# Turning q and k of two first blocks on quarters of the array, with their loads and two M1 chunks moved

## The chip, the cores and the metric

The kernel runs on one core of one Trainium2 chip. Its time is the device time of an execution in microseconds (us). Of the kernel before, three runs are shown; the median is 339.99 us. The engines are PE (TensorE, the 128x128 matmul array, with its weight loads shown as PEld), DVE (VectorE), ACT (ScalarE), POOL (GpSimd) and SP (SyncE, which here only issues DMAs). The pages' "L583" is line 583 of the kernel before.

## What is computed

For 8 batches, 8 heads, 576 positions and 64 values a head, a causal attention with forgetting, and then a two-layer SiLU network on the 4608 rows of 512 values:

```python
scores = scale * np.matmul(q, k.transpose(0, 1, 3, 2))
cum = np.cumsum(np.log(np.clip(f, 0.0001, 1.0)), axis=-1)
decay = cum[:, :, :, None] - cum[:, :, None, :]
scores = np.where(causal, -1000000000.0, scores + decay)
attn = softmax(scores)
x = (attn @ v), heads side by side          # 4608 x 512
h = x @ w_in                                # 512 x 2048
out = (h / (1 + exp(-h))) @ w_out           # 2048 x 512
```

The forgetting factor of the key is folded into v (and into a column of ones beside it, which gives the denominators); that of the query cancels in the division.

## The kernel before

**Two kinds of attention work.** The first 128 positions of each batch are its *first block*. They are worked on ahead of everything else, a whole batch of 8 heads at once: `load_qk0` (two POOL-queue DMAs per batch, one for q and one for k, each 128 rows of 512 values, cast to bf16 on the way, row = 16 position groups x 8 heads), `turn0` (turns them so that the head's 64 values lie on the partitions), `scores0`, `mask0`, `out0`, `back0`. Positions 128 to 575 are worked on in the main loop in 32 *pairs* of heads: `load_qk`, `cast_qk` (POOL), a DMA transpose on SP's queue (`transposes`, L443), `scores` (L475), `mask`, `attend` (L522, L531), `back`.

**`turn0`** takes q or k of one batch. For each of 8 positions c in a group and each j of two head halves it does one matmul (L293): the 128 rows x 64 values as weights, a 128x64 selection matrix `sel[:, j, :]` as the moving operand, the result on partitions 64j to 64j+63 of a tile `tp` in the PSUM pool `pbig` (4 buffers of one bank, shared with the tiles of M1, M2 and others). ACT copies q's tile out to `qT0`, DVE copies k's to `kT0`. A batch has 32 of these matmuls. The score tiles are in another PSUM pool, `psc` (2 buffers of two banks).

**M1 and M2** are the two layers of the network. The rows are cut into 10 groups; group 0 is the first blocks of batches 0 to 3 (512 rows), groups 1 and 2 those of batches 4, 5 and 6, 7 (256 rows each). An M1 chunk (`m1_chunk`, L583) is 4 matmuls, tanh on ACT (L591) and one DVE operation (L592); a group has 16. An M2 part (`m2_part`, L628) is 4 matmuls of 512 columns on a quarter of w_out; four parts make 128 rows of output, which ACT scales (L638) and SP stores (L607). In the main loop some M2 work has another form (`m2_rows`, L654).

**What sets the order.** All engines run in the order in which the program is written. Between the pieces of attention, `fill(us)` asks a planner (`wanted`, `plan`) for M1 chunks and M2 parts worth so many microseconds by the planner's own costs, and `step(kind)` asks for one. Before the main loop the order is: turns of batches 0 to 3 and their attention; M1 chunks of group 0; `two_more(4)` (turns, scores, output of batches 4 and 5, with fills between); a list of kinds written out by hand (1 is an M1 chunk, 2 an M2 part); `fill(2.2)`; `two_more(6)`; stores and loads; `fill(4.2)`; the main loop. `two_more(6)` begins with four `turn0`, then two steps of fill, then `scores0` of both batches.

**The loads.** Two queues matter. POOL's, in this order: q and k of the first blocks, v of them, w_in in quarters, w_out in quarters (`load_w_out(0)` to `(3)`), with POOL's own conversions of v (`convert_v0`) between them; the last ones before the main loop are `load_qk0(6)`, `load_qk0(7)`, `load_v0(6)`, `load_v0(7)`. And SP's: everything for the main loop. SP's queue begins with `after(...)` (L211), a tiny DMA that waits for the second quarter of w_out; then q, k, tails, transposes, v and stores in the program's order.

Of the kernel before, what the change touches and what calls it, by code (L numbers as in the profile page):

```python
# [10 lines left out]
FP32 = mybir.dt.float32  # L11
BF16 = mybir.dt.bfloat16
P = 128
# [5 lines left out]
def kernel(  # L19
# [10 lines left out]
    nc = tc.nc  # L30

    B, H, S, D = q.shape
# [4 lines left out]
    NP = H // 2  # L37
# [10 lines left out]
    RUN = 8  # L48
    NRUN = P // RUN
    assert D == 64 and S == 576 and DM == H * D and NP == NCC and B == 8  # L50
    assert NRUN * H == P
    scale = 1.0 / float(D) ** 0.5

    ctx.enter_context(tc.manual_schedule(engines=set(ORDERED)))
# [1 line left out]
    const = ctx.enter_context(tc.tile_pool(name="const", bufs=1))  # L56
    stage = ctx.enter_context(tc.tile_pool(name="stage", bufs=1))
    conv = ctx.enter_context(tc.tile_pool(name="conv", bufs=6))
    qktp = ctx.enter_context(tc.tile_pool(name="qktp", bufs=4))
# [8 lines left out]
    psc = ctx.enter_context(tc.tile_pool(name="psc", bufs=2, space=bass.MemoryType.PSUM))  # L68
# [4 lines left out]
    w_bf = const.tile([P, NM + 1, BH], BF16, name="w_bf")  # L73
    ident_bf = const.tile([P, P], BF16, name="ident_bf")
    sel = const.tile([P, 2, D], BF16, name="sel")
    ident_f = const.tile([BH, BH], FP32, name="ident_f")
    tri = const.tile([P, P], BF16, name="tri")
    trit = const.tile([P, 2, ST], BF16, name="trit")
# [4 lines left out]
    kT0 = [const.tile([P, NP, P], BF16, name=f"kT0_{b}") for b in range(B)]  # L83
# [46 lines left out]

    def load_qk0(b):
        t = conv.tile([P, 2, RUN * D], BF16, name="qkb", tag="qkb")
        for i, src in enumerate((q, k)):
            nc.gpsimd.dma_start(
                out=t[:, i, :],
                in_=src[b, :, 0:P, :].rearrange("h (r c) d -> r h (c d)", c=RUN),
            )
        qk0[b] = t

    def load_v0(b):  # L140
# [62 lines left out]
    def load_w_out(i):  # L203
        c0, c1 = i * NFC // WQ, (i + 1) * NFC // WQ
        nc.gpsimd.dma_start(
            out=w_out_bf[:, c0:c1, :],
            in_=moe_w_out[c0 * P : c1 * P, :].rearrange("(fc p) m -> p fc m", p=P),
        )
# [22 lines left out]
    for i in range(2):  # L231
        nc.vector.tensor_copy(
            out=sel[:, i, :].rearrange("p (a r) -> p a r", a=NP),
            in_=ident_bf[:, :].rearrange("p (r i a) -> p i a r", i=2, a=NP)[:, i, :, :],
        )

    def keep_warm(n):
# [7 lines left out]
        out=f_sb[:, :], in0=f_sb[:, :], scalar1=1e-4, scalar2=1.0, op0=ALU.max, op1=ALU.min  # L245
# [39 lines left out]
    def turn0(b, i):  # L285
        src = qk0[b]
        if i == 0:
            qT0[b] = qktp.tile([P, NP, P], BF16, name="qT0", tag="qT0", bufs=2)
        dst, evac = ((qT0[b], nc.scalar.copy), (kT0[b], nc.vector.tensor_copy))[i]
        tp = pbig.tile([P, NP, NRUN, RUN], FP32, name="tp", tag="big")  # L290
        for c in range(RUN):
            for j in range(2):
                nc.tensor.matmul(  # L293
                    tp[j * D : (j + 1) * D, :, :, c].rearrange("p a r -> p (a r)"),
                    lhsT=src[:, i, c * D : (c + 1) * D],
                    rhs=sel[:, j, :],
                    start=True,
                    stop=True,
                )
        evac(  # L300
            out=dst[:, :, :].rearrange("p a t -> p (a t)"),
            in_=tp[:, :, :, :].rearrange("p a r c -> p (a r c)"),
        )
# [43 lines left out]
    def convert_v0(b):  # L347
        nc.gpsimd.tensor_tensor(
            out=v0[b][:, :, :],
            in0=vf0.pop(b)[:, :, :],  # L350
            in1=w_bf[:, 0, b * H : (b + 1) * H, None].to_broadcast([P, H, D + 1]),
            op=ALU.mult,
        )
# [85 lines left out]
    def transposes(n):  # L439
        src = qbf.pop(n)  # L440
        t = qktp.tile([P, NX, P], BF16, name="qkT", tag="qkT")
        qkT[n] = t[:, :, :].rearrange("p x c -> p (x c)")
        nc.sync.dma_start_transpose(  # L443
            out=t[:, :, :], in_=src[:, :, :].rearrange("p x c -> p (x c)")
        )
# [130 lines left out]
    def m1_chunk(g, fc):  # L576
        w = GW[g]
        if fc == 0:
            gts[g] = gpools[g % 3].tile([P, NFC, w], BF16, name="gt", tag=f"gt{g % 3}")
        gt = gts[g]  # L580
        hp = pbig.tile([P, w], FP32, name="hp", tag="big")
        for cc in range(NCC):
            nc.tensor.matmul(  # L583
                hp[:, :],
                lhsT=w_in_bf[:, cc, fc * P : (fc + 1) * P],
                rhs=xcols(g, cc),
                start=(cc == 0),
                stop=(cc == NCC - 1),
            )
        th = tpool.tile([P, w], BF16, name="th", tag="th")  # L590
        nc.scalar.activation(out=th[:, :], in_=hp[:, :], func=ACT.Tanh, scale=0.5)  # L591
        nc.vector.scalar_tensor_tensor(  # L592
            out=gt[:, fc, :],
            in0=th[:, :],
            scalar=1.0,
            in1=hp[:, :],
            op0=ALU.add,
            op1=ALU.mult,
        )
# [95 lines left out]
    def wanted(a, c):  # L695


        g1 = M1[a][0] if a < len(M1) else NG
        g2 = M2[c][0] if c < len(M2) else NG
        can1 = g1 in ready and not (M1[a][1] == 0 and g1 > g2 + lag["g"])  # L700
        can2 = open2["w"] and c < len(M2) and g2 < g1
        if can1 and can2 and lag["parts"]:
            return 2 if sum(M2_OF[:g1]) - c > lag["parts"] else 1
        if not can1 or not can2:
            return 1 if can1 else 2 if can2 else 0
        a0, c0 = begin.get(g1, (M1[a][1], c)) if M1[a][1] else (0, c)
        c1 = sum(M2_OF[:g1])
        f1 = (M1[a][1] - a0 + 0.5) / (NFC - a0)
        f2 = (c - c0 + 0.5) / max(1, c1 - c0)
        return 1 if f1 <= f2 else 2  # L710

    def step(force=0):

        a, c = at["m1"], at["m2"]
        want = wanted(a, c)
        if not want:
            return None
        g1 = M1[a][0] if a < len(M1) else NG
        g2 = M2[c][0] if c < len(M2) else NG
        can1 = g1 in ready and not (M1[a][1] == 0 and g1 > g2 + lag["g"])  # L720
        can2 = open2["w"] and c < len(M2) and g2 < g1
        kind = force if (force == 1 and can1) or (force == 2 and can2) else want
        if kind == 1:
            if M1[a][1] == 0:
                begin[g1] = (0, c)
            m1_chunk(g1, M1[a][1])
            at["m1"] += 1
            t = 4 * (GW[g1] / 2.4 + 2.5)
        else:
            m2_part(*M2[c])  # L730
            at["m2"] += 1
            t = 4 * (DM / 2.4 + 2.5)
        return t
# [20 lines left out]
    def fill(us_, least=0, ends=(0, 0)):  # L754

        left = us_ + at["left"]
        kinds = plan(left)
        kinds += [0] * (least - len(kinds))
        if any(ends) and kinds:
            if 2 not in kinds:  # L760
                kinds[0] = 2
            n1, n2 = len(kinds) - kinds.count(2), kinds.count(2)
            e0 = 1 if ends[0] else 0
            e1 = 1 if ends[1] and n2 > e0 else 0
            inner = n2 - e0 - e1
            n = n1 + inner
            mid = [2 if (x + 1) * inner // n > x * inner // n else 1 for x in range(n)]
            if inner and mid[-1] == 2 and e1 and not e0:
                mid = mid[::-1]
            kinds = [2] * e0 + mid + [2] * e1  # L770
        for k in kinds:
            t = step(k)
            if t is None:
                at["left"] = 0.0
                return
            left -= t / 1000
        at["left"] = left
# [48 lines left out]
    for i in range(2):  # L826
        r = slice((1 - i) * ST, (2 - i) * ST)
# [2 lines left out]
        nc.gpsimd.memset(t[:, 0:NM, 1, :], 0.0)  # L830
    load_w_out(0)
    load_w_out(1)
    convert_v0(4)
    convert_v0(5)
    load_w_out(2)
    load_w_out(3)
    load_qk0(6)
    load_qk0(7)
    load_v0(6)
    load_v0(7)  # L840
# [11 lines left out]
    cast_qk(1)  # L852
    transposes(1)

    def two_more(b):
        for x in range(2):
            turn0(b + x, 0)
            turn0(b + x, 1)
        fill(1.2, 2)
        for x in range(2):  # L860
            scores0(b + x)
            mask0(b + x)
        fill(2.6 if b == 4 else 3.4, 3)
        out0(b)
        fill(0.6, 1)
        out0(b + 1)
        fill(0.8, 2)
        back0(b, on_act)
        fill(0.6, 1)
        back0(b + 1, on_act)  # L870
        if b == 4:
            open2["w"] = True
            step(2)
        else:
            fill(0.6, 1)
# [1 line left out]
    fill(5.9)  # L877
    two_more(4)
    ready.add(1)
    for kind in (1, 1, 2, 1, 1, 2, 1, 1, 1, 1, 2):  # L880
        assert step(kind) is not None
    at["left"] = 0.0
    begin[M1[at["m1"]][0]] = (M1[at["m1"]][1], at["m2"])
    fill(2.2)
    two_more(6)
    ready.add(2)
    store(len(stores))
# [6 lines left out]
    for c in range(NM):  # L894
        convert_v(0, c)
    fill(4.2)

# [80 lines left out]
    for m in range(NQ):  # L980
# [19 lines left out]
        if m > 0:  # L1000
            if m % 2 == 0:
                b = m // 2 - 1
# [90 lines left out]
```

## Time and profile before

| | us |
|---|---|
| three runs | 340.03, 339.99, 338.6 (median 339.99) |
| the profiled execution | 341.14 |
| its span, first to last instruction | 339.4 |
| PE busy | 326.7 |
| ACT, DVE, POOL busy | 217.2, 200.5, 139.5 |
| granted PE clock | 0.999 |

A timeline row gives the start in us, the time covered, the engine, the line, the operation with its operands (out<-in), and how many instructions were merged; in square brackets, the engine's idle time before it and what ended it. "SPq" is SP's queue issuing a DMA. Rows of the chain of waits give start, duration, and what the end of the program hung on at that time. In the page's second part each digit stands for a fortieth of the span, 8.5 us, and gives the busy share in tenths. The trace also has each DMA's landing, from the semaphore that it raises; where a text gives a landing, it is that record.

The stretches that matter here, in us from the span's start: first blocks of batches 0 to 3 until 18.6; M1 of group 0 and batches 4 and 5 until 37.5; M1 of group 1 with M2 of group 0 and, from 47.4, batches 6 and 7, until 62.4; then the main loop.

### The profile page before, as it was taken

How to read it: one execution, taken by the hardware profiler on the slowest of the kernel's cores; microseconds unless marked ns; L12 is line 12 of the kernel's file. 1: busy time of each engine (PE TensorE's matmuls, PEld its weight loads, DVE VectorE, ACT ScalarE, POOL GpSimd, SP SyncE). 2: the span in 40 equal slices, each digit the busy share in tenths (PEclk: the TensorE clock that was granted, in tenths of full speed). 3: DMA queues.
4: the chain of work that ended last, by engine and by line, in shares of the span. 5: the costliest groups of instructions: out<-in, count | busy, mean ns of one | idle time of the engine just before them, and what ended most of it. 6: DMA issues, size and time to landing. Idle time of an engine off the chain costs nothing.

```text
span 339.4 us, 10334 instructions
## 1 busy us (share of the span) xinstructions
PE 326.7 (96%) x4268; PEld 229.2 (68%) x4292; DVE 200.5 (59%) x435; ACT 217.2 (64%) x385; POOL 139.5 (41%) x223
## 2 busy tenths in 40 slices
PE   7999999999999999999999997999999999999995
PEld 3745566798786767758857894867676676555654
DVE  4668745369568467565656965886673557344330
ACT  5767546687777577758748792866776486344431
POOL 8894426574764664464474352628060000000000
PEclk9999999999999999999999999999999999999999
DMA  8999999999999998997999789959973110001012
GB/s 155 187 189 220 180 215 164 241 171 172 182 188 170 168 186 158 194 190 150 181 179 165 147 148 147 156 115 188 151 108 87 53 38 33 34 33 59 34 62 63
DMA packets 144703, 48.01 MB, mean 141 GB/s; under 512 B 133328, under 2 KB 139728, under 8 KB 144656
## 3 DMA queue, kind: packets, MB, share of 16 engines
q1 hardware_dynamic: 115088, 36.60, 56.9%
q0 software_dynamic: 29408, 10.62, 27.0%
q8 instruction: 33, 0.54, 0.7%
q10 hardware_dynamic: 160, 0.13, 0.2%
q14 instruction: 14, 0.11, 0.1%
HBM read 36.85 MB, written 9.44 MB: 136 GB/s over the span
## 4 chain that ended last, share of the span: by engine, by line
PE 85%; DMA 6%; DVE 4%; POOL 2%; issue 1%; ACT 1%; SPq 1%; POOLq 0%
PE hp L583 33%; PE po L628 20%; PE pr L654 15%; PE sc L475 6%; PE dn L522 5%; DMA vf<-in_v_dram 3%; PE dn L531 2%; DMA qkb<-in_k_dram 1%; PE tp L293 1%; DVE gt L592 1%; DMA qf<-in_q_dram 1%; DVE ut L498 1%; DVE u L343 1%; SPq L443 1%; POOL vp L429 1%
## 5 line engine op out<-in xcount | busy, mean ns | idle before, releaser
L591 ACT ACTIVATE th<-hp 128x384 bf16<-128x384 f32 (+2 forms) x208 | 96.5, 468 | 75.0 <-PE hp L583 68.8
L592 DVE SCALAR_TENSOR_TENSOR gt<-th,hp 128x384 bf16<-128x384 bf16 (+2 forms) x208 | 107.5, 523 | 54.3 <-ACT th L591 44.3
L583 PE MATMUL hp<-x,w_in_bf 128*128 128x384 bf16 (+2 forms) x701 | 120.6, 321 | 0.7 <-DVE gt L592 0.4
L583 PEld LDWEIGHTS <-w_in_bf 128*128 128x128 bf16 x832 | 79.0, 98 | 50.2 <-issue 3.7
L486 ACT ACTIVATE u<-sc 128x1024 bf16<-128x1024 f32 (+1 forms) x96 | 74.3, 811 | 6.9 <-PE sc L475 6.9
L628 PE MATMUL po<-w_out_bf,gt 128*128 128x512 bf16 (+1 forms) x316 | 74.1, 368 | 1.4 <-DVE gt L592 0.2
L654 PE MATMUL pr<-w_out_bf,gt 64*128 64x256 bf16 x1024 | 61.4, 269 | 0.0
L409 POOL CAST qkb<-qf 128x384 bf16<-128x384 f32 x32 | 17.3, 542 | 88.9 <-DMA qf<-in_q_dram 88.3
L654 PEld LDWEIGHTS <-gt 64*128 64x128 bf16 x1024 | 51.2, 94 | 3.9
L628 PEld LDWEIGHTS <-gt 128*128 128x128 bf16 x336 | 32.2, 98 | 27.4 <-issue 0.3
L160 POOL DMA_DIRECT2D qkb<-in_k_dram x56 | 43.9, 786 | 0.8 <-issue 0.7
L429 POOL TENSOR_TENSOR vp<-vf,w_bf 128x520 bf16<-128x520 f32 (+1 forms) x40 | 36.5, 915 | 14.0 <-DMA vf<-in_v_dram 11.9
L638 ACT ACTIVATE osb<-po 128x512 f32<-128x512 f32 (+1 forms) x21 | 12.1, 577 | 26.5 <-PE po L628 26.5
L475 PE MATMUL sc<-qkT 64*128 64x128 bf16 (+1 forms) x640 | 28.2, 206 | 0.4 <-DMA qkT<-qkb 0.3
L492 DVE TENSOR_TENSOR u<-u,tri 128x768 bf16<-128x768 bf16 x32 | 20.2, 631 | 13.5 <-ACT u L486 13.5
L475 PEld LDWEIGHTS <-qkT 64*128 64x128 bf16 x640 | 20.3, 94 | 7.6 <-issue 4.7
L480 ACT ACTIVATE ut<-sc 128x640 bf16<-128x640 f32 x32 | 22.4, 701 | 3.0 <-PE sc L475 2.5
L522 PEld LDWEIGHTS <-u 128*128 128x128 bf16 x576 | 20.6, 97 | 3.1
L522 PE MATMUL dn<-vp,u 128*128 128x65 bf16 x384 | 21.8, 193 | 0.0
L540 DVE TENSOR_TENSOR xr<-dn,rec 128x448 bf16<-128x448 f32 x32 | 20.0, 625 | 1.1
L522 PE MATMUL dn<-v,u 128*128 128x65 bf16 x192 | 20.0, 194 | 0.0
L665 DVE COPY fence<-pr 128x1 f32<-128x1 f32 x16 | 2.5, 158 | 28.0 <-PE pr L654 28.0
(70 smaller groups left out, 243.4 us busy)
## 6 DMA issues: line engine op xcount, KB each, us to landing
out_dram<-osb SPq DMA_DIRECT2D x32, 256.0 KB, 2.9
vf<-in_v_dram SPq DMA_DIRECT2D x26, 256.0 KB, 5.1
qf<-in_q_dram SPq DMA_DIRECT2D x64, 96.0 KB, 3.3
qkb<-in_k_dram POOLq DMA_DIRECT2D x56, 48.0 KB, 4.0
w_in_bf<-in_moe_w_in_dram POOLq DMA_DIRECT2D x4, 512.0 KB, 6.8
w_out_bf<-in_moe_w_out_dram POOLq DMA_DIRECT2D x4, 512.0 KB, 9.1
vf<-in_v_dram POOLq DMA_DIRECT2D x6, 256.0 KB, 9.6
qkb<-in_q_dram POOLq DMA_DIRECT2D x8, 128.0 KB, 4.9
```

Source lines behind the costliest of these rows:

```text
L160: nc.gpsimd.dma_start(out=t2[:, NR + 1 : NX, j * D : (j + 1) * D], in_=k[b, head(p, j), P:SM, :].rearrange("(c p) d -> p c d", p=P),)
L429: nc.gpsimd.tensor_tensor(out=vbf[b][ro, c, ho, :], in0=vst[b][c][r, h, :], in1=w.to_broadcast([r.stop - r.start, h.stop - h.start, D + 1] ...
L475: nc.tensor.matmul(sc[:, i, o : o + q1 - q0], lhsT=kt, rhs=t[r, q0:q1], start=True, stop=True)
L480: nc.scalar.activation(out=ut[:, :, 0:3:2, :].rearrange("p k i t -> p i k t"), in_=sc[:, :, T0 : T0 + (NM + 1) * ST].rearrange("p i (k t) ...
L486: nc.scalar.activation(out=u[:, :, c * SM : c * SM + w], in_=sc[:, :, 0:w], func=ACT.Exp, scale=scale)
L492: nc.vector.tensor_tensor(out=x, in0=x, in1=tri[:, None, None, :].to_broadcast([P, 2, NR, P]), op=ALU.mult)
L522: nc.tensor.matmul(dn[:, i * NR + c - 1, :], lhsT=u[:, i, o : o + P], rhs=vals(kb, i), start=(kb == 0), stop=(kb == c),)
L583: nc.tensor.matmul(hp[:, :], lhsT=w_in_bf[:, cc, fc * P : (fc + 1) * P], rhs=xcols(g, cc), start=(cc == 0), stop=(cc == NCC - 1),)
L591: nc.scalar.activation(out=th[:, :], in_=hp[:, :], func=ACT.Tanh, scale=0.5)
L592: nc.vector.scalar_tensor_tensor(out=gt[:, fc, :], in0=th[:, :], scalar=1.0, in1=hp[:, :], op0=ALU.add, op1=ALU.mult,)
L628: nc.tensor.matmul(po[:, :], lhsT=gt[:, fc, tb * P : (tb + 1) * P], rhs=w_out_bf[:, fc, m0:m1], start=(fc == 0), stop=(fc == NFC - 1),)
L654: nc.tensor.matmul(pos[g, tb][y], lhsT=gt[r, fc, tb * P : (tb + 1) * P], rhs=w_out_bf[r, fc, y * DM // 2 : (y + 1) * DM // 2], start=(half ...
```

## The change

- For batches 6 and 7 the DMAs are cut in two: q goes to partitions 0 to 63 and k to partitions 64 to 127 of the same tile, four heads in each of two columns of it. Four DMAs of 64 rows take the place of two of 128.
- For these two batches `turn0` gives way to `turn0_quarters`: 32 matmuls a batch as before, each with 64 rows and 64 columns, in the order q half 0, k half 0, q half 1, k half 1. The result is one tile in the score pool `psc` (a bank for q, a bank for k) instead of two tiles in `pbig`. The moving operand is `selh`, 128x64, made once by two DVE copies.
- `load_qk0(6)` is issued after the second quarter of w_out and ahead of `convert_v0(4)`, instead of after the fourth quarter.
- The hand-written list before `two_more(6)` has two more M1 chunks, the fill behind it asks for 1.8 instead of 2.2, and one `step(1)` is added ahead of the main loop.

The diff, cut to its core:

```diff
-        for i, src in enumerate((q, k)):
-            nc.gpsimd.dma_start(
-                out=t[:, i, :],
-                in_=src[b, :, 0:P, :].rearrange("h (r c) d -> r h (c d)", c=RUN),
-            )
+        for z, src in enumerate((q, k)):
+            if b < 6:
+                nc.gpsimd.dma_start(
+                    out=t[:, z, :],
+                    in_=src[b, :, 0:P, :].rearrange("h (r c) d -> r h (c d)", c=RUN),
+                )
+                continue
+            for i in range(2):
+                nc.gpsimd.dma_start(
+                    out=t[z * D : (z + 1) * D, i, :],
+                    in_=src[b, i * NP : (i + 1) * NP, 0:P, :].rearrange(
+                        "a (r c) d -> r a (c d)", c=RUN
+                    ),
+                )
...
     load_w_out(0)
     load_w_out(1)
+    load_qk0(6)
     convert_v0(4)
     convert_v0(5)
     load_w_out(2)
     load_w_out(3)
-    load_qk0(6)
     load_qk0(7)
...
+    for z in range(2):
+        r = slice(z * D, (z + 1) * D)
+        nc.vector.tensor_copy(
+            out=selh[r, :].rearrange("p (a r) -> p a r", a=NP),
+            in_=ident_bf[r, r].rearrange("p (r a) -> p a r", a=NP),
+        )
+
+    def turn0_quarters(b):
+        qT0[b] = qktp.tile([P, NP, P], BF16, name="qT0", tag="qT0", bufs=2)
+        sc = psc.tile([P, 2, NP, NRUN, RUN], FP32, name="tq", tag="sc")
+        for c in range(RUN):
+            for j in range(2):
+                for i in range(2):
+                    r = slice(i * D, (i + 1) * D)
+                    nc.tensor.matmul(
+                        sc[j * D : (j + 1) * D, i, :, :, c].rearrange("p a r -> p (a r)"),
+                        lhsT=qk0[b][r, j, c * D : (c + 1) * D],
+                        rhs=selh[r, :],
+                        start=True,
+                        stop=True,
+                    )
+        for i, (dst, evac) in enumerate(
+            ((qT0[b], nc.scalar.copy), (kT0[b], nc.vector.tensor_copy))
+        ):
+            evac(
+                out=dst[:, :, :].rearrange("p a t -> p (a t)"),
+                in_=sc[:, i, :, :, :].rearrange("p a r c -> p (a r c)"),
+            )
...
-            turn0(b + x, 0)
-            turn0(b + x, 1)
+            if b == 4:
+                turn0(b + x, 0)
+                turn0(b + x, 1)
+            else:
+                turn0_quarters(b + x)
...
-    for kind in (1, 1, 2, 1, 1, 2, 1, 1, 1, 1, 2):
+    for kind in (1, 1, 2, 1, 1, 1, 1, 2, 1, 1, 1, 1, 2):
...
-    fill(2.2)
+    fill(1.8)
...
     fill(4.2)
+    step(1)
```

Followed through the planner's arithmetic, the steps around the turns of batches 6 and 7 come in this order (M1 g c is chunk c of group g; M2 g t p is part p of the t-th 128 rows of group g):

| | before | after |
|---|---|---|
| by the hand-written list | M1 1 0 to 1 7, M2 0 0 1 to 0 0 3 | M1 1 0 to 1 9, M2 0 0 1 to 0 0 3 |
| then | M2 0 1 0, M1 1 8, M2 0 1 1, M1 1 9 | M2 0 1 0, M1 1 10, M2 0 1 1 |
| turns of 6 and 7, then | M2 0 1 2, M2 0 1 3 | M2 0 1 2, M1 1 11 |
| scores0 of 6 and 7, then until the main loop | M1 1 10 to 1 15, M2 to 0 3 3 | M1 1 12 to 1 15, M2 to 0 3 3, M1 2 0, M1 2 1 |
| main loop | M1 2 0 and on | M1 2 2 and on; the same order from pair 4 on |

More of the change, by code (lines that the diff above doesn't have):

```diff
@@ L50 @@
     assert D == 64 and S == 576 and DM == H * D and NP == NCC and B == 8
-    assert NRUN * H == P
+    assert NRUN * H == P and NRUN * NP == D
     scale = 1.0 / float(D) ** 0.5
@@ L75 @@
     sel = const.tile([P, 2, D], BF16, name="sel")
+    selh = const.tile([P, D], BF16, name="selh")
     ident_f = const.tile([BH, BH], FP32, name="ident_f")
```

## The prediction

> **What bounds the kernel now.** I read the page first, then PE's timeline around the changed turns, then the chain of waits after them, and last the DMA queues.
>
> ```profile
> span 339.4 us, 10334 instructions
> PE 326.7 (96%) x4268; PEld 229.2 (68%) x4292; DVE 200.5 (59%) x435; ACT 217.2 (64%) x385; POOL 139.5 (41%) x223
> DMA  8999999999999998997999789959973110001012
> ```
>
> PE is busy for 96% of the span, but in the first two thirds the DMA engines are full as well (9 tenths in nearly every slice of 8.5 us). So two limits lie side by side there, and a PE microsecond counts only where PE doesn't wait for a load soon after. The profiled execution took 341.14 us, 1.74 more than its span of 339.4; the median of the runs is 339.99. I sum in the profiled execution and carry the difference over to the median.
>
> PE around the turns of blocks 6 and 7:
>
> ```profile
> 46.85 0.60 PE L583 MATMUL hp<-x,w_in_bf 128*128 128x256 bf16 x4
> 47.38 2.08 PE L293 MATMUL tp<-sel,qkb 128*64 128x64 bf16 x64
> 49.62 1.67 PE L628 MATMUL po<-w_out_bf,gt 128*128 128x512 bf16 x7 [0.16 <-issue]
> 51.23 0.62 PE L327 MATMUL sc<-qT,kT 64*128 64x128 bf16 x16
> ```
>
> Two M2 parts of 4 matmuls follow the turns, but 7 of the 8 are recorded: the missing first one began one start-to-start of 512 columns (0.216 us) earlier, at 49.40. The 64 turning matmuls thus cost 49.40 - 47.38 = 2.02 us. No load is waited for before them: the last load of q and k landed at 44.96 by the trace's landing records.
>
> The next place where PE does wait for a load, and the chain behind it:
>
> ```profile
> 86.32 0.28 PE L475 MATMUL sc<-qkT 64*128 64x64 bf16 x8
> 86.87 0.40 PE L475 MATMUL sc<-qkT 64*128 64x128 bf16 x8 [0.28 <-DMA qkT<-qkb]
> ```
>
> SP's queue before it, and four pieces of the chain of waits:
>
> ```profile
> 74.91 0.52 SPq L607 DMA_DIRECT2D out_dram<-osb  x1
> 75.48 1.03 SPq L169 DMA_DIRECT2D qf<-in_q_dram  x2
> 76.55 0.62 SPq L179 DMA_DIRECT2D qktf<-in_q_dram  x1
> 77.22 0.63 SPq L179 DMA_DIRECT2D qktf<-in_k_dram  x1
> 77.89 1.77 SPq L190 DMA_DIRECT2D vf<-in_v_dram  x2
> 79.84 3.06 SPq L443 DMA_TRANSPOSE qkT<-qkb  x1
> ```
>
> ```profile
> 75.17 0.23 DVE ut L498
> 75.41 0.02 SPq L607
> 82.94 4.83 DMA vf<-in_v_dram
> 90.51 0.19 PE dn L531
> ```
>
> At 86.87 PE waits 0.28 us for the DMA transpose of pair 5, which landed at 86.83, and at 90.51 attend waits 0.18 us for v. The chain of waits ties this load chain to PE through a store (L607) at 75.41. I don't believe that link: the store was issued at 74.91 and took 0.52 us, what such an issue takes anyway, and DVE had finished the tile it stores by 68.1. What I see instead, going back: the transpose landed behind v (84.62), which is ahead of it in the same queue; SP could issue all this only after the transpose of pair 4 at 73.44, which waited for k of pair 4 (landed 73.30); POOL had issued that k at 68.47, behind its conversions of v, and that v had landed at 64.23 behind full DMA engines. So from 36 to 87 us the loads go by their own clock.
>
> **The change, part by part.** *Quarters.* Per block 32 matmuls stay 32 matmuls of 64 columns, but each now fills 64 rows instead of 128. Before, two column halves start together every 0.056 us by the trace's starts: 32 pairs x 0.056 = 1.79; the closing switch of the array's form takes 0.10 and a wait for a PSUM buffer about 0.1 more, together the 2.02 us. Row halves are shown to run side by side: the 64x64 group at 86.32 takes 0.28 with 0.19 for one (the row at 86.29 in the timeline), so (0.28 - 0.19)/7 = 0.013 us each. Row halves and column halves are both shown; both at once are not. Upper bound: nothing overlaps further, 1.79, saved 0.1 (the buffer wait goes). Lower bound: four at once with the 0.028 of two fast row halves, 16 x 0.028 = 0.45, saved 1.5. I take four per 0.056, i.e. 0.014 each, nearest to the row of 0.013: 0.90 + 0.10 = 1.00, **saved 1.02 us**.
>
> One rule speaks against it: the Trainium skill, "TensorE: Matmul & The Clock Gate", section "Wait — 56ns, not 53.3ns?", says that matmuls never start less than about 25 ns apart however short they are. By that, an estimate from the page, the turns would cost 64 x 0.025 = 1.6 and save 0.3. The 0.013 us above contradicts it for tiles in different halves.
>
> *Evacuation.* q takes ACT 0.59 and k takes DVE 0.69, as before. The last one of block 7 ends about 2.0 us after the turns begin (0.9 + 0.2 until the matmuls are out, then DVE's second 0.69 behind its first); scores of block 6 need only block 6's, 0.7 earlier, and come 1.0 + 0.86 + 0.44 = 2.3 us after. Cover is 1 us. The score buffers that the turns borrow were last read by DVE after out0(5), by 36.9; the scores need them back only when their operands are ready anyway.
>
> *selh.* Two DVE copies; the two for sel took 0.27 and 0.21. DVE idles from 18.79 to 20.28 at that point, so nothing; 0.5 if that cover were gone.
>
> *Loads.* q and k of blocks 6 and 7 become eight DMAs of 64 rows instead of four of 128: four more POOL issues, at most 0.55 each, 2.2 us. Those of block 6 fall into the 4.4 us in which POOL waits for v (until 29.75). POOL's DMAs use eight semaphores in turn, so the fourth waits for the last w_in quarter (landed 28.45), still ahead of 29.75. Those of block 7 now wait for w_out's second quarter (35.66) and block 6's (about 37.4), so v of block 7 is issued near 39 instead of 37.7; the queue ahead of it is full until 43. The third and fourth quarter of w_out landed at 38.78 and 41.51 and now stand behind block 6's bytes (41.51 to 43.22, 1.71 us): 40.5 and 43.2. Before, M2 used them at 40.99 and 43.82. Two M1 chunks (0.44 each) put M2's third part at 41.86, the fourth at 44.46: 1.3 and 1.2 us to spare, no wait. SP's loads wait for w_out's second quarter, which is ahead of all this, so they start at 35.67 as before.
>
> *M1 chunks.* By the planner's arithmetic 12 chunks of group 1 instead of 10 precede the turns, and two chunks of group 2 precede the main loop; attention pairs 0 to 3 then run with the same number of chunks between them, and the last gap before pair 4 has four instead of six. From pair 4 on the order is the same to the end.
>
> **The sum.** PE reaches the turns 0.87 us later, leaves them 0.15 earlier, keeps this through pairs 0 to 3, and reaches scores of pair 5 at 86.59 - 1.02 = 85.57. There the transpose lands at 86.83, since nothing on its chain has moved: the one store on it that needs PE's work (its output tile finished at 57.87) was issued at 58.70 with 0.8 us to spare. PE's wait grows from 0.28 to 1.3, and what was saved is given back whole. After 90.5 the same work follows in the same order. Sum: 0 in 341.14, and at most -0.17 if the store's time does matter. **339.9 us.**
>
> **The rivals.**
> *The loads follow PE* (the chain of waits is right at 75.41, or DMA engines freed by other timing bring the transpose forward). Then the 1.02 stays: 339.0, or 338.5 with the best pace. For: the profile draws that link. Against: the store's ordinary 0.52.
> *Half-width loads cost full price*: slower. One DMA of 128 rows takes 0.87 us of the queue (42.34 to 43.22). If one of 64 rows takes the same, each block's loads take 3.5 instead of 1.74: w_out's third quarter lands at 42.3 and M2 waits 0.4, and all loads behind come up to 3.5 us late, less some 2.1 that slices with free DMA time give back (0.36 of the engines busy in 54 to 55, 0.63 in 69 to 70). PE then waits 1.4 to 3.5 at pairs 0 to 5: about 342.3. It decides from about 0.3 us more per DMA, a quarter of M2's spare 1.3. For: v loads of 64 rows take 5.7 us to land against 5.1 for whole ones. Against: q and k tails, also 64 rows, follow each other at 0.63 for 128 KB.
> The Trainium skill, "SBUF — State Buffer", section "Door 1: The DMA port swizzle", speaks for this rival: 64 partitions reach half of the ports, 196 against 328 GB/s. The 128-row DMA here writes 128 KB in 0.87 us, 147 GB/s, below either figure, so by it no wait arises.
> *The late DVE stall moves.* At 202.99 one mask_tail takes 2.78 us where the median is 0.23, beside POOL's v conversion, and PE then waits 2.24 at 206.15, its longest wait. If timing shifts, it may go: 337.7. Against: the waits at 86.8 and 90.5 bring PE, POOL and loads back to the same spacing.
> *The quarters don't overlap*: saved 0.1, PE 0.8 late through pairs 0 to 3, but still at 86.5 for the transpose: 339.9 too.
>
> **How the numbers follow.** Forecast 0.60, quarters without overlap 0.05, loads follow PE 0.15, half-width loads 0.11, stall gone 0.09. Half a per cent is 1.7 us, about what a measurement can tell: faster by more than that 0.09, slower 0.11, within 0.80. The likeliest's own range is 339.4 to 340.4. The range leaves out the stall and most of the half-width case: from 338.4 (loads follow, best pace) to 341.5 (the foot of half-width).
>
> **What would show it.** Turning matmuls in about 1.0 us from their first start to the next M2 part; scores of pair 0 near 62.2; a wait of about 1.3 us for qkT at 86.8 in place of 0.28. Wrong if that wait ends a microsecond earlier, if M2 waits for w_out near 42, or if the 2.24 us wait near 206 is gone or has a twin.

## The result and the profile after

The median of 22 runs after the change is 338.06 us (336.73 to 340.01); the kernel before, run beside it, has 339.73 (22 runs, 338.6 to 341.62). Medians and ratios, here and below, leave out the few executions over 1.5% slower than the fastest of their kernel. The ratio is 0.995 with a 95% interval of 0.9935 to 0.9966: 1.67 us or half a per cent faster, 0.3 us below the stated range. The profiled execution took 340.01 us and is the slowest of the 22, so the profile is read for where time goes, and the medians for how much. The page's first and second part:

```profile
span 337.9 us, 10342 instructions
PE 327.3 (97%) x4269; PEld 228.7 (68%) x4292; DVE 197.9 (59%) x437; ACT 217.4 (64%) x385; POOL 141.7 (42%) x227
DMA  8999998999999995999999979959963110011012
```

PE's busy time and the DMA digits have hardly moved; nothing on this page says what became faster. PE's timeline at the changed turns and at pair 5:

```profile
46.36 1.03 PE L638 MATMUL po<-w_out_bf,gt 128*128 128x512 bf16 x4
47.32 1.09 PE L879 MATMUL tq<-selh,qkb 64*64 64x64 bf16 x64
48.57 0.81 PE L638 MATMUL po<-w_out_bf,gt 128*128 128x512 bf16 x3 [0.16 <-issue]
...
87.34 0.40 PE L485 MATMUL sc<-qkT 64*128 64x128 bf16 x8 [1.31 <-DMA qkT<-qkb]
```

The first of the four M2 matmuls behind the turns has no record; it began 0.216 us earlier, at 48.35. The turns cost 48.35 - 47.32 = 1.03 us instead of 2.02. The main loop's first scores begin at 61.77 (62.37 before). Then PE's waits from 60 to 110 us (total, times, longest):

```profile
PE sc L485 <- DMA qkT<-qkb: 2.2, 2, 1.3
PE dn L541 <- POOL vp L439: 0.5, 1, 0.5
```

Before, the same view has 0.3 and 0.2. The two waits for transposes are at pair 3 (74.57, about 0.95) and at pair 5 (the last row above); the transpose of pair 5 landed at 87.29, against 86.83 before. At the attend of 90.5, now at 91.31, PE is 0.8 us later than before. All this is one execution; the second profile of the same kernel (e5, below) has other waits. What makes this profiled execution 1.13 us shorter all the same is another place: the wait of 2.24 us near 206 is gone.

Theories to test: the turns' saving stays; the moved loads bring something forward; the stall near 206 was the gain; the M1 chunks. The expectations give what each would make of a run.

### The profile page after: what moved, and what is told of

Same layout as the page of the kernel before. It is cut to its first block, busy times and chain, and to the rows that moved or that the text cites. A ratio compares the mean times of both kernels' runs of the same rounds, so it can differ in the third digit from the quotient of the medians.

```text
span 337.9 us, 10342 instructions
## 1 busy us (share of the span) xinstructions
PE 327.3 (97%) x4269; PEld 228.7 (68%) x4292; DVE 197.9 (59%) x437; ACT 217.4 (64%) x385; POOL 141.7 (42%) x227
## 4 chain that ended last, share of the span: by engine, by line
PE 73%; DMA 10%; SPq 9%; POOL 5%; issue 1%; ACT 0%; DVE 0%; POOLq 0%
PE hp L593 29%; PE po L638 16%; PE pr L664 13%; PE sc L485 6%; PE dn L532 5%; DMA w_out_bf<-in_moe_w_out_dram 4%; SPq L179 3%; DMA vf<-in_v_dram 3%; PE dn L541 2%; SPq L453 2%; SPq L189 2%; PE wm L250 1%; DMA qkb<-in_k_dram 1%; DMA kf<-in_k_dram 1%; SPq L200 1%
## 5 line engine op out<-in xcount | busy, mean ns | idle before, releaser
L502 DVE TENSOR_TENSOR u<-u,tri 128x768 bf16<-128x768 bf16 x32 | 21.8, 681 | 14.0 <-ACT u L496 13.9
```

What stands on the lines that cost most here:

```text
L502: nc.vector.tensor_tensor(out=x, in0=x, in1=tri[:, None, None, :].to_broadcast([P, 2, NR, P]), op=ALU.mult)
```

## The experiments

Each line has the median of up to 12 runs (up to 10 for the last), that of the kernel before run beside it, and the ratio with its 95% interval. "Filled" is explained under "What the load move does".

| run | us | before | ratio |
|---|---|---|---|
| e1, quarters alone | 339.12 | 339.40 | 0.9990 (0.9954 to 1.0027) |
| e2, load move alone (filled) | 338.43 | 339.40 | 0.9964 (0.9940 to 0.9987) |
| e3, chunks alone | 340.24 | 339.40 | 1.0019 (0.9989 to 1.0048) |
| e4, changed kernel with 1.08 us of PE work added | 338.41 | 339.40 | 0.9982 (0.9951 to 1.0013) |
| e5, changed kernel again | 338.35 | 339.35 | 0.9965 (0.9943 to 0.9987) |
| e6, changed kernel without quarters (filled) | 338.09 | 339.35 | 0.9969 (0.9945 to 0.9993) |
| e7, changed kernel without chunks (filled) | 337.87 | 339.35 | 0.9947 (0.9920 to 0.9975) |
| e8, before without the late conversions | 339.47 | 339.35 | 0.9996 (0.9972 to 1.0020) |
| e9, w_out's third quarter sooner (filled) | 338.44 | 339.51 | 0.9974 (0.9950 to 0.9999) |
| e10, both quarters sooner (filled) | 338.47 | 339.51 | 0.9980 (0.9956 to 1.0003) |
| e11, changed kernel, v of batch 1 not loaded | 337.15 | 339.51 | 0.9934 (0.9911 to 0.9956) |
| e12, the same without quarters | 337.89 | 339.51 | 0.9972 (0.9942 to 1.0002) |
| e13, quarters with e10's order (filled) | 338.00 | 339.48 | 0.9958 (0.9944 to 0.9972) |
| e14, e13 with SP's loads sooner (filled) | 337.86 | 339.48 | 0.9949 (0.9919 to 0.9979) |
| e16, cut loads alone | 340.17 | 339.39 | 1.0029 (0.9993 to 1.0065) |

**The parts one by one.** e1 has only the quarters with their cut loads; e2 only the load of block 6 moved; e3 only the chunks; e4 is the changed kernel with `keep_warm(5)`, 1.08 us of dummy matmuls, behind the turns of block 7.

```diff
# e1, against after; list, fill(2.2) and no step(1) as before
-    load_qk0(6)
     convert_v0(4)
     convert_v0(5)
     load_w_out(2)
     load_w_out(3)
+    load_qk0(6)
# e2, against before: the same move, the other way
# e3, against before
-    for kind in (1, 1, 2, 1, 1, 2, 1, 1, 1, 1, 2):
+    for kind in (1, 1, 2, 1, 1, 1, 1, 2, 1, 1, 1, 1, 2):
...
-    fill(2.2)
+    fill(1.8)
...
+    step(1)
# e4, against after, in two_more, behind the turns
+        if b == 6:
+            keep_warm(5)
```

> Quarters and the cut loads alone; load order and M1 chunks as before. T1 (on record: the loads of the main loop keep their own clock and PE's saving is given back as a wait): within 0.3 us of before. T2 (in an ordinary execution the loads don't bind and the 1.0 us that the turns save stays): 0.8 to 1.2 us faster than before. T3 (what counts is whether the mask_tail of about 203 us stalls DVE for some 2.7 us and PE for 2.2): about 2 us faster if its profile lacks that stall, about 0 if it has it.

> The load of q and k of batch 6 ahead of the third and fourth quarter of w_out alone, everything else as before. T1 and T2: same as before within 0.3 us (M2 waits up to 0.2 us for w_out at most). T3: 0 or about -2 us, as its profile shows the late stall or not.

> The two M1 chunks moved alone, with the shorter fill and the added step. T1: the pairs 0 to 3 run 0.9 us later against their loads, no wait that isn't there before: within 0.3 us. T2: the same, or up to 0.5 us faster if the loads of pairs 0 to 3 are what PE waits for in an ordinary execution. T3: 0 or about -2 us with the late stall.

> The changed kernel with five 512-column matmuls of zeros behind the turns of batch 7, 1.08 us of PE (they leave the result alone). T1: within 0.3 us of the changed kernel, since PE waits for the loads at pair 5 anyway. T2: 0.9 to 1.2 us slower than the changed kernel, some 0.6 faster than before. T3: back to before if the late stall returns, else like T1 or T2.

The edit that was costed at nothing, the load move, gives 0.97 us alone; the quarters alone, costed at 1.02 saved, give 0.28, which can't be told from zero. e1's profile shows one possible reason. POOL's timeline:

```profile
40.36 0.50 POOL L142 DMA_DIRECT2D qkb<-in_k_dram  x1 [3.00 <-DMA w_out_bf<-in_moe_w_out_dram]
43.71 0.50 POOL L142 DMA_DIRECT2D qkb<-in_k_dram  x1 [2.85 <-DMA w_out_bf<-in_moe_w_out_dram]
```

and PE's at the turns:

```profile
49.94 0.63 PE L879 MATMUL tq<-selh,qkb 64*64 64x64 bf16 x29 [2.22 <-DMA qkb<-in_k_dram]
```

POOL's DMAs use eight semaphores in turn (the trace's records go through the same eight again and again), so with twice as many DMAs for q and k POOL stands 3.00 and 2.85 us until w_out's third and fourth quarter have landed, issues block 7's k late, and PE waits 2.22 us in the middle of the turns. After them this profile has no wait for a load from 60 to 110 us.

e1's zero isn't firm, though, as a reading made after the runs shows. In four of its twelve runs the granted clock over the span is 0.993 to 0.995, and these are its four longest. The other eight have a median of 338.66 us, against 339.40 for the 31 runs of before with 0.997 or more: 0.74 us faster. That lower clock arises ahead of everything that the change touches: in the profiles with 0.995 (e3, e9, e16, e17) it was 0.50 to 0.54 from 20 to 22 us and 1.00 from 24 us on.

The chunks alone show no gain. With e4's padding the profile has no wait for a load from 60 to 110 us at all; its median is 0.35 us above the changed kernel's first one and 0.06 above e5's, its ratio 0.003 (1.1 us) and 0.002 (0.6 us) above, and the intervals overlap. So it stays open how much of the padding the loads take up.

**The changed kernel, less one part.** e5 is the changed kernel once more, e6 has the load move and the chunks without quarters, e7 all but the chunks.

```diff
# e6, against before: the edits of e2 and of e3
# e7, against after: the edits of e3 undone
```

> The changed kernel once more, beside the others of this call. All theories: 0.994 to 0.997 of before, as measured (338.06 against 339.73). T1 (loads bind, saving given back): its profile has a wait of over 1 us for a transposed q and k at pair 3 or 5. T2 (an ordinary execution keeps the 1.0 us): the same kernel may show such a wait in its profile, but its fastest runs lie 1.0 us below those of before. T3 (the DVE stall at about 203 us): no mask_tail of over 1 us there.

> The changed kernel without the quarters: loads moved (whole DMAs) and chunks moved, old turns. T1: within 0.3 us of the changed kernel. T2: 0.9 to 1.1 us slower than the changed kernel. T3: like the changed kernel if its profile has no late stall, up to 2 us slower if it has one.

> The changed kernel without the moved M1 chunks (old list, fill and no added step): quarters, cut loads, loads moved. M2 then reaches the third quarter of w_out at about 40.5 and the fourth at 43.4, which landed at 40.3 and 43.4 in the changed kernel. All theories: up to 0.5 us of waits for w_out; T1: within 0.4 us of the changed kernel, T2: 0 to 0.5 us slower, since the chunks only cover that wait.

e5 gains 1.00 us, but its profile lacks the wait of over 1 us that T1 asked for. PE's waits in it from 60 to 110 us:

```profile
PE dn L541 <- POOL vp L439: 0.5, 1, 0.5
PE sc L485 <- DMA qkT<-qkb: 0.4, 1, 0.4
```

The transpose of pair 5 landed at 85.86, 1.4 us sooner than in the first profile of the very same kernel. The other profiles with quarters (e1, e4, e7, e13, e14, e17) have no such wait for a transpose at all, and of the kernels without quarters e2, e6 and e10 have one of 0.8 to 0.9. So the 1.31 us belong to one execution.

e6 keeps most of the gain (1.26 us), and e7 loses none. What the chunks cover is small; PE's waits of e7 from 36 to 60 us:

```profile
PE po L638 <- DMA w_out_bf<-in_moe_w_out_dram: 0.3, 2, 0.2
```

**The late stall.** e8 is the kernel before with POOL's v conversions of batch 6 left out (its output uses the values of batch 4 there), so that DVE's mask_tail near 203 has nothing beside it.

```diff
 def convert_v(b, c):
     vbf[b] = vps[b % 2]
+    if b == 6:
+        return
```

> The kernel before, without POOL's conversion of v of batch 6 (left out: the values of batch 4 are used in its place), so that the mask_tail of about 203 us has no POOL work to be stalled by. T3: about 1.5 to 2.2 us faster than before, if before has the stall in most runs. T1 and T2: at most 0.5 us faster, since a stall that comes and goes with the run can't be the difference of two medians.

The wait near 206 is gone in its profile and the time is that of before, 339.47 against 339.35: this theory falls. The 2.78 us belong to before's profiled execution, which at 341.14 is 1.4 us above before's median; they are not what its runs usually pay.

**What the load move does.** The windows view gives, per stretch, busy time of PE, PEld, DVE, ACT and POOL, then granted clock, DMA share and GB/s. Before:

```profile
34.00:38.00 4.00, 3.46 (x21) 1.48 (x20) 3.93 (x9) 2.68 (x6) 3.65 (x6) 1.00 1.17 171
38.00:42.00 4.00, 4.00 (x29) 2.62 (x28) 2.32 (x6) 1.76 (x5) 0.00 (x0) 1.00 1.19 186
```

After:

```profile
34.00:38.00 4.00, 3.93 (x25) 2.03 (x24) 3.89 (x8) 2.74 (x5) 2.31 (x5) 1.00 1.25 204
38.00:42.00 4.00, 3.89 (x29) 2.73 (x28) 2.12 (x6) 2.31 (x6) 2.06 (x3) 1.00 1.22 196
```

The DMA share hardly differs, 1.17 and 1.25, and both make a 9 in the page's digits. The bytes do: 171 against 204 GB/s, with 206 just before (30 to 34). There is a hole in the load queue, and POOL's timeline of before shows what opens it:

```profile
29.75 2.51 POOL L348 TENSOR_TENSOR v<-vf,w_bf 128x520 bf16<-128x520 f32 x2 [4.42 <-DMA vf<-in_v_dram]
32.20 1.55 POOL L205 DMA_DIRECT2D w_out_bf<-in_moe_w_out_dram  x2
33.74 0.55 POOL L134 DMA_DIRECT2D qkb<-in_q_dram  x1
```

w_out's third and fourth quarter stand behind two conversions that wait 4.42 us for v, so they are issued at 32.20 while what was queued before lands by 35.66. In the changed kernel four DMAs are in the queue before the conversions:

```profile
25.14 1.05 POOL L142 DMA_DIRECT2D qkb<-in_q_dram  x2
26.35 0.50 POOL L142 DMA_DIRECT2D qkb<-in_k_dram  x1 [0.16 <-issue]
29.04 0.50 POOL L142 DMA_DIRECT2D qkb<-in_k_dram  x1 [2.19 <-DMA w_in_bf<-in_moe_w_in_dram]
```

They landed at 36.79 to 37.79, right behind w_out's second quarter (36.45). If the hole is the cause, anything else issued ahead fills it as well, without block 6, quarters or chunks. e9 and e10 do that:

```diff
# e9 (e10 moves load_w_out(3) as well), against before
+    load_w_out(2)
     convert_v0(4)
     convert_v0(5)
-    load_w_out(2)
     load_w_out(3)
```

> The kernel before with one line moved: the third quarter of w_out is issued ahead of POOL's conversions of v of batches 4 and 5. Nothing else. T4 (new: in the kernel before POOL's load queue runs short between 34 and 41 us, because the third quarter of w_out is issued only after the conversions; what is issued ahead of them fills that hole, whatever it is, and all later loads come 0.8 to 1.5 us earlier, which PE gets because it waits for them at pairs 3 to 5): 0.8 to 1.5 us faster than before, about 204 GB/s in 34 to 38 us instead of 171. Rival T5 (what counts is that q and k of batch 6 come early): same as before within 0.4 us.

> The kernel before with both the third and the fourth quarter of w_out ahead of the conversions. T4: as e9_third_quarter or up to 0.3 us better, without any wait for w_out. T5: same as before within 0.4 us.

e9's windows and its POOL timeline:

```profile
34.00:38.00 4.00, 3.52 (x30) 1.68 (x28) 3.97 (x8) 2.50 (x6) 4.00 (x8) 1.00 1.23 204
38.00:42.00 4.00, 3.81 (x24) 2.13 (x24) 3.18 (x7) 2.27 (x5) 0.82 (x1) 1.00 1.25 206
```

```profile
25.75 2.25 POOL L205 DMA_DIRECT2D w_out_bf<-in_moe_w_out_dram  x3
31.66 2.51 POOL L348 TENSOR_TENSOR v<-vf,w_bf 128x520 bf16<-128x520 f32 x2 [3.66 <-DMA vf<-in_v_dram]
```

One line moved, a different load, and the same: 204 GB/s and 1.07 us (1.04 for e10, whose interval just takes in no change). So the gain doesn't need block 6 to come early. Over 34 to 38 the trace gives 171, 139 and 147 GB/s for before, e1 and e8, which leave the hole open (e3, also open, 194 there and 189 in the next four), and 198 or more for every kernel with a filled one. The depth of the open hole follows the moment at which w_out's third quarter is issued: 31.75 us and 194 GB/s in e3, 32.20 and 171 in before, 32.79 and 155 in e15, 32.98 and 147 in e8 (e1, at 32.78 and 139, lies a little off). From the landing of w_out's second quarter to that of POOL's last load (v of block 7) it takes 12.04, 11.93, 13.17 and 12.57 us in before, e3, e8 and e15, and 11.20 to 11.81 in after, e2, e6, e9 and e10.

**What the quarters are worth.** e11 and e12 leave out the load of v of batch 1 in the main loop (their outputs are computed with stale v there), so that loads don't bind PE at pairs 3 to 5; e11 has the quarters, e12 not. e13 and e14 join the quarters to the other way of filling the hole, e14 with SP's loads let go at w_out's first quarter.

```diff
# e11 against after, e12 against e6, in load_v(b, c)
+    if b == 1:
+        vst[b].append(t)
+        return
# e13, against e1: load_w_out(2) and (3) ahead of convert_v0(4)
# e14, against e13
-    after(w_out_bf[0:1, 2 * NFC // WQ - 1, DM - 16 : DM])
+    after(w_out_bf[0:1, NFC // WQ - 1, DM - 16 : DM])
```

> The changed kernel with the SP loads of v of batch 1 left out (the values of batch 0 stand in for them), 1 MB less between 75 and 90 us, so that PE has no load to wait for at pairs 5 and on. T1 (the quarters save 1.0 us of PE, which is given back because the loads bind): 0.8 to 1.2 us faster than e12_no_quarters_no_v1, and its profile has no load wait over 0.3 us after 80 us. Rival: the quarters save nothing even then: the two within 0.4 us.

> The changed kernel without the quarters (loads and chunks moved), with the SP loads of v of batch 1 left out in the same way. T1: 0.8 to 1.2 us slower than e11_after_no_v1, though the two kernels with these loads are within 0.4 us of one another. Both should be 0.5 to 2 us faster than before.

> Quarters with cut loads, the third and fourth quarter of w_out ahead of POOL's conversions, block 6's loads not ahead and no M1 chunk moved: e10_both_quarters with quarters. T4 with T1 (the filled hole is the gain, the quarters' 1.0 us is still given back at the loads of pairs 3 to 5): 1.0 to 1.4 us faster than before, like the changed kernel. Rival (the quarters' 1.0 us adds to the filled hole): 2.0 to 2.4 us faster than before. In both the turns of block 7 don't wait for their loads, as they did by 2.2 us in e1_quarters.

> e13_quarters_filled with SP's loads of the main loop let go at the first quarter of w_out instead of the second, about 2 us sooner. T4 with T1 (PE waits for these loads at pairs 3 to 5, so loads that start sooner let PE keep part of the quarters' 1.0 us): 0.3 to 1.0 us faster than e13_quarters_filled, load waits over 0.3 us gone at 74 to 91 us. Rival (the stream is held by what the DMA engines carry in all, so an earlier start only takes their time from w_out and block 7): within 0.3 us of e13_quarters_filled, or slower by a wait for w_out or for v of block 6.

With loads out of the way the quarters bring 337.89 - 337.15 = 0.74 us of their 1.0 by the medians, 1.3 by the ratios, with overlapping intervals. With loads in place and the hole filled, the four kernels without quarters (e2, e6, e9, e10) gain 1.09 us in the mean of their medians, the five with them (after, e5, e7, e13, e14) 1.45, which makes 0.4; the mean ratios are 0.9972 and 0.9954, which makes 0.6. Averaged over the single runs it is 1.0 us without (48 runs) and 1.5 with (68). So the quarters keep 0.4 to 0.6 us, with overlapping intervals. None of e7, e13 and e14 can be told from the changed kernel, and e14 not from e13.

In e13, with the same cut loads as e1 and the hole filled, the turns don't wait. In e14 they do, by 1.36 us for block 7's k, and yet e14's median is as good as e13's. So a wait at the turns alone doesn't decide the time, and e1's smaller gain isn't fully explained by it.

**Where a part of the quarters' saving goes.** The time of an execution less its span is 1.76 to 1.80 us in the mean of every kernel without quarters up to here, e12 apart, and 2.06 to 2.08 in every one with them, e11 apart. Three kernels look for the cause: the copies of selh alone, the cut loads alone, and the quarters for block 7 only.

```diff
# e15, against before: the two tensor_copy that make selh, nothing else
# e16, against before, in load_qk0
+            for z in range(2 if b >= 6 else 1):
+                w = P // 2 if b >= 6 else P
+                nc.gpsimd.dma_start(
+                    out=t[z * w : (z + 1) * w, i, :],
...
# e17, against after
-            if b < 6:
+            if b < 7:
...
-            if b == 4:
+            if b + x < 7:
```

> The kernel before with the two DVE copies that make selh, and nothing that uses it. Asked is the time outside the span (time of an execution less its span): 1.76 to 1.80 us in every kernel so far without the quarters, 2.06 to 2.08 in every one with them. If a tile or two DVE instructions more are what sets it: 2.07. If it hangs on the DMAs or the matmuls: 1.78. The span itself should be that of the kernel before, 337.7, within a microsecond.

> The kernel before with only the loads of q and k of blocks 6 and 7 cut into halves of 64 rows (same layout, same turns, same place in the queue): four more POOL DMAs. If the DMAs set the time outside the span: 2.07, otherwise 1.78. Inside the span POOL now waits for landings of w_out before the later of these DMAs, as in the run with the quarters alone, and the load queue runs emptier: PE waits for block 7's q and k at its turns, by 2.2 us there. If later waits for loads swallow that, the time is that of the kernel before, 339.5; if not, up to 341.5.

> The changed kernel with block 6 loaded and turned in the old way and only block 7 by quarters (two more DMAs than before instead of four). Time outside the span: near 1.92 if each DMA or each quarter matmul adds its share, 2.07 if the form of the program counts and not the number, 1.78 if neither. The turns of both blocks: 1.0 (old form) + 0.5 us.

Outside the span are 1.82 us in e15, 2.07 in e16 and 2.00 in e17: the cut DMAs make the 0.29 us, not the copies, and two more make most of what four make, so neither the proportional 1.92 nor the all-or-nothing 2.07 was met. It isn't simply their number either: e12, with four DMAs fewer than e6, has 2.00. What decides stays open. Inside the span e16 widens the hole, as its windows show, and its turns wait:

```profile
34.00:38.00 4.00, 3.82 (x34) 2.05 (x33) 3.93 (x9) 2.25 (x5) 4.00 (x6) 1.00 0.89 134
38.00:42.00 4.00, 3.93 (x25) 2.21 (x24) 3.21 (x6) 2.64 (x6) 2.47 (x6) 1.00 1.14 171
```

```profile
51.35 0.64 PE L297 MATMUL tp<-sel,qkb 128*64 128x64 bf16 x16 [0.56 <-DMA qkb<-in_k_dram]
```

Its median is 0.78 us above before, e1's 0.28 below; with only the runs whose granted clock is 0.997 or more it is 0.46 above (5 runs) and 0.74 below (8). So by the medians the cut loads cost something in this order and the turns more than pay it back, though e16's interval still takes in no change. e15 (338.62) and e17 (338.80) ran once each.

## Why the prediction was right and where it was wrong

**Turns: right.** 1.00 predicted, 1.03 measured; 64 matmuls of 64x64 start four per 0.056 us, 3 to 4 ns apart within a four. The Trainium skill's floor of about 25 ns between starts ("TensorE: Matmul & The Clock Gate", "Wait — 56ns, not 53.3ns?") would have made them 1.6 us, an estimate from the page; these matmuls on different quarters go against it, at 0.014 us each. The rival without overlap falls with that measurement.

**Evacuation, selh, M2: right.** Scores of pair 0 came at 61.77 (near 62.2 predicted), in part by luck: this execution had begun M2 of group 0 at 36.82 instead of 37.52, and so PE reached the turns at 47.32 and not 0.87 us later than before. w_out's last quarters landed at 40.33 and 43.40 (40.5 and 43.2 predicted) and M2 did not wait for them. With the two chunks M2 had 1.0 and 0.8 us to spare (1.3 and 1.2 predicted); without them, in e7, it waited 0.3.

**Half-width loads: right in the queue, not free.** Block 6's four DMAs took 36.45 to 37.79, 1.34 us; e2's two whole ones 36.29 to 37.63, also 1.34. The slower rival had no ground. 256 KB (262144 bytes) in 1.34 us are 196 GB/s (by the same count the 147 GB/s of the prediction are 151). The Trainium skill ("SBUF — State Buffer", "Door 1: The DMA port swizzle") has the same 196 for 64 partitions, but as whole loads to 128 partitions took no less here, no run shows the ports to be the limit. What I missed is that each extra DMA takes one of eight semaphores, which I saw for block 6 and did not follow to block 7 without the load move (e1), and that the cut loads add 0.29 us outside the span, which I never counted.

**Loads: the step that failed.** The sum put the move of block 6's loads at nothing. "The queue ahead of it is full until 43" and "nothing on its chain has moved" treated the move of block 6's loads as a mere reordering of bytes that flow without a gap. I had read "the DMA engines are full" from digits of busy share; cut finer, 34 to 38 us carried 171 GB/s where 204 were to be had. The page's next row even has the drop, 180 in the fifth slice between 220 and 215:

```profile
GB/s 155 187 189 220 180 215 164 241 171 172 182 188 170 168 186 158 194 190 150 181 179 165 147 148 147 156 115 188 151 108 87 53 38 33 34 33 59 34 62 63
```

From 34 to 42 that is (33 + 10) x 4 = 172 KB not moved, at 204 GB/s 0.84 us. The edit I costed at nothing gives 1.0 us alone and 1.3 with the chunks (e2, e6); e9 and e10 get as much by another load.

**Giving back: the other step that failed.** "What was saved is given back whole" doesn't hold once the hole is filled: of the 1.0 us, 0.4 to 0.6 stays in the time and 0.3 goes outside the span, so at most 0.1 to 0.3 is left for waits, less than these runs can tell. The wait at pair 5 did grow from 0.28 to 1.31 in the profile after, as predicted to the tenth, but that was luck: it is the slowest of the 22 runs, the second profile of the same kernel has 0.43, and the profiles of e1, e4, e7, e13, e14 and e17 have none. How much is given back while the hole is open stays undecided: e1 gains 0.28 us, or 0.74 in the runs with a clock of 0.997 or more.

**The rivals.** "The loads follow PE" (339.0) named the right sign, and part of its 1.02 does stay; but most of the gain comes from a hole that it didn't see, and whether PE's store ever releases the loads wasn't tested. "The stall goes" (337.7) has the profile of after on its side and is refuted by e8: two single profiles differed there, two sets of runs did not.

**Still open.** The chain from the filled hole to the end is argued, not shown. The sooner landing of POOL's last load is in the traces, but the profiled executions scatter by about a microsecond: from the start of M1 to the first scores of pair 6 PE took 77.27 to 78.41 us in before, e1, e3, e8 and e15, 77.41 to 78.21 in e2, e6, e9 and e10, and 76.39 to 78.39 in after, e5, e7, e13 and e14. The means are 77.93, 77.87 and 77.09: at that place the profiles show 0.8 us for the quarters and nothing yet for the filled hole alone, where the medians say 0.4 to 0.6 and 1.1. The bytes tell the same: e2, e6, e9 and e10 have moved their first 9 MB 27.8 us after M1's start, against 28.7 in before, e3, e8 and e15, but their first 15 MB no sooner (60.6 in both). In e13 and e14, whose cut loads wait for w_out again, POOL's last load even lands 14.3 and 14.8 us after the second quarter, and they gain all the same. So that filling the hole gains a microsecond rests on the medians of four kernels, with three different edits, that have only this in common; how it reaches the end is open. It isn't that POOL gets its issues done sooner: its last load of v is issued at 36.57, 36.20, 37.88 and 35.95 in e2, e6, e9 and e10 and at 39.13 in after, against 36.71 in before.

## What to carry to other kernels

A DMA busy share near its ceiling doesn't say that the queue is full: read GB/s in the same stretch against the best stretch nearby, and where it drops, look for compute on the engine that issues the loads. An edit that only moves loads can't be taken as free of effect until each queue has been followed from issue to landing on both sides of the move. Where one profile differs from another by a single long wait, test it by a run without it before believing it; and where a wait comes out as predicted, take a second profile of the same kernel (here 1.31 us, then 0.43). Splitting a DMA has a price of its own in the semaphores that limit how far ahead the engine can issue.

## What the runs showed of the hardware

Two surprises. First, the share of busy DMA engines fell only from 1.25 to 1.17 where the bytes fell from 204 to 171 GB/s. Second, a small DVE operation can take twelve times its usual time beside POOL's work. In before's DVE timeline mask_tail, 0.23 us in the median:

```profile
202.99 2.78 DVE L498 TENSOR_TENSOR ut<-ut,trit 128x128 bf16<-128x128 bf16 x1
```

and POOL beside it:

```profile
202.02 1.56 POOL L160 DMA_DIRECT2D qkb<-in_k_dram  x2
203.60 2.08 POOL L429 TENSOR_TENSOR vp<-vf,w_bf 128x520 bf16<-128x520 f32 x2
```

It began during POOL's DMA issue and ended with POOL's conversions. In after's DVE timeline the same operation is short:

```profile
203.88 0.58 DVE L508 TENSOR_TENSOR ut<-ut,trit 128x128 bf16<-128x128 bf16 x1
```

There POOL's conversions began at 204.59, 0.71 after it; in before 0.61 after it. In e4 it took 1.64. In e8, which leaves these conversions out, it took 0.22. The order of work around it is the same in before, after and e4. That POOL holds it is thus likely, not shown; what decides between 2.78 and 0.58 wasn't tried, and the two starts differ by 0.1 us.
